# Old output form for the first eight groups, earlier scores for the next batch, and filler matmuls in the head of an inducing-point attention + PReLU expert kernel

## The chip, the cores and the metric

The kernel runs on one core of one Trainium2 chip. The metric is the device time of one execution in microseconds (us). The engines are named as in the profile: PE (TensorE matmuls), PEld (TensorE weight loads), DVE (VectorE), ACT (ScalarE), POOL (GpSimd), SP (SyncE, which here only issues DMAs). A name such as `ring<-rep,hW` means that an instruction writes tile `ring` and reads `rep` and `hW`.

## The reference, cut to what matters

```python
B, N, m, C = (4, 12480, 32, 128)          # x is (B, N, C), inducing is (m, C)
def mab(q, kv):
    s = scale * (q @ kv.transpose(0, 2, 1))
    a = exp(s - s.max(-1)); a /= a.sum(-1)
    return a @ kv
h = mab(I, x)                             # 32 inducing points look at 12480 tokens
x = mab(x, h).reshape(B * N, C)           # every token looks at the 32 points
hid = x @ w_in                            # 128 -> 2048
g = max(hid, 0) + alpha * min(hid, 0)     # PReLU, one alpha for each of the 2048
out = g @ w_out                           # 2048 -> 128, float32
```

## The kernel before, in words

**Tiling.** A batch of 12480 tokens is six supergroups of 2048 tokens and a remainder of 192. A supergroup is four groups of 512, so a batch has 25 groups, and each group passes through four slots `j` (the remainder through two). I write (b, g) for group g of batch b and (b, g, j) for a slot. There are 392 slots in all, and the main loop at the end of the kernel takes them in order. `base = 25 * b` is the number of a batch's first group.

**One slot.** `fill` issues four matmuls that use 32 rows of the array each (`ring<-rep,hW`: the unnormalised attention weights of 512 tokens, kept in `rep`, times the product of the points and `w_in`, kept in `hW`) into four of six PSUM banks called `ring`. ACT (line 470) and DVE (line 472) evict these four banks with a ReLU into `gt`; which engine takes which bank is decided ahead by `make_plan`, a beam search with a cost for every instruction. After that the second matmuls of the slot before are issued by `mm2` into one of two accumulators `acc`. The linear part of the PReLU comes from two small matmuls for a pair of groups (`linear`).

**Two output forms.** `turned(b, g)` chooses between them. In the turned form `mm2` issues four matmuls that stream 512 tokens through weights `W1`, and the result has channels on the partitions. `turn` then transposes blocks on DVE into `yT` (line 563), sixteen DMAs for a supergroup that POOL issues (line 572) shuffle `yT` to `yq`, POOL multiplies by the reciprocal row sums `rd` (line 579) and issues the DMA to `out` (line 589). POOL's sixteen shuffles and four such closings wait in a list `moves`, from which the main loop takes two in a slot. In the old form `mm2` issues sixteen matmuls that load 128 tokens of `gt` as weights and stream 128 columns of `W1`; the tokens are on the partitions at once, and `finish` needs one DVE multiplication (line 548, tile `obe`) and one DMA to `out`. Before the change the old form is used for the last supergroup of the last batch and for the four remainders.

**The next batch's first attention** is interleaved as tasks placed with `at(slot, fn, j)`. For each supergroup u of batch n: `a_load` (POOL issues a casting DMA to `xn`, line 133), `a_xpose` (SP issues a DMA transpose `xT<-xn`, line 158), `a_scores` (PE: `ring<-xT,IT`; ACT: exponential to `e1`; SP: DMA transpose `e1T<-e`, line 281) and `a_accum`, the pooling (PE: sixteen matmuls `ring<-xn,e1T`; DVE adds them to `hacc`). The group in which scores are issued is `t`, the pooling comes at `t + d`, and the load and the transpose at `k` and `k + 1`:

```python
if b == 0:
    k, t, d = (1, 3, 4, 5, 7, 9, 11)[i], (8, 9, 11, 13, 15, 16, 17)[i], 2
else:
    k, t, d = base + (-8, -5, -3, -2, 1, 4, 7)[i], base + (0, 2, 4, 7, 10, 13, 16)[i], 3
```

The index i runs over the supergroups in the order 0, 1, remainder, 2, 3, 4, 5. `e1` and `e1T` come from a pool of two buffers.

**Order.** `pin` chains every instruction to the one before it on its engine, so each engine works in the order in which the code is written, and so does each engine's DMA queue. SP's queue holds, in one order, the transposes of `xn`, those of `e1`, and the copies `e2d<-e` and `rep<-e2d` that spread a supergroup's attention weights.

**The head.** Batch 0's first attention runs ahead of the main loop in halves of a supergroup: PE transposes (`p_xpose`), scores (`p_scores`) and pooling (`p_pool`) into columns 0 to 31 of `acc` 0. Then follow `p_sums`, `p_h`, `p_scale` (row sums and `hT`), `b_scores_pe`, `h_weights` and `b_scores`, which make the first group's `rep` and `hW`.

Of the kernel before, what the change touches and what calls it, by code (L numbers as in the profile page):

```python
# [15 lines left out]
P = 128  # L16
NB = 4
GRP = P * NB
NQ = 4
# [5 lines left out]
def kernel(  # L25
# [11 lines left out]
    bf16 = mybir.dt.bfloat16  # L37
# [5 lines left out]
    NS = N // SUP  # L43
# [31 lines left out]
    gt_pool = ctx.enter_context(tc.tile_pool(name="gtp", bufs=4))  # L75
    head_pool = ctx.enter_context(tc.tile_pool(name="headp", bufs=3))
    rep_pool = ctx.enter_context(tc.tile_pool(name="repp", bufs=3))
    rd_pool = ctx.enter_context(tc.tile_pool(name="rdp", bufs=4))
    dram = ctx.enter_context(
        tc.tile_pool(name="e2d", bufs=3, space=bass.MemoryType.DRAM)  # L80
# [124 lines left out]
    def p_scores(st, u, i):  # L205
        blocks = p_blocks(st, u, i)
        pp, nb = (PR, JR) if u == NS else (P, 2 * NB)
        ps = bank()
        for k, (xt, _) in enumerate(blocks):
            mm(ps[:pp, k * M : (k + 1) * M], xt, IT[:])  # L210
        e1t = head_pool.tile([P, 2 * NB, M], bf16, name="e1t", tag="e1t")
        pin(nc.scalar.activation(  # L212
            out=e1t[:pp, :nb, :].rearrange("p k m -> p (k m)"), in_=ps[:pp, : nb * M],
            func=EXP, scale=scale,
        ))
        st.e1T[u, i] = e1t

    def p_pool(st, u, i, first=False, last=False):
        blocks = p_blocks(st, u, i)
        pp, nb = (PR, JR) if u == NS else (P, 2 * NB)  # L220
        e1t = st.e1T.pop((u, i))
        step = min(4, nb)
        for k in range(0, nb, step):
            mm(
                den[: step * M, :], e1t[:pp, k : k + step, :].rearrange("p k m -> p (k m)"),
                ones[:pp, :], start=(first and k == 0), stop=(last and k + step == nb),
                skip_group_check=True,
            )
        for k, (_, xk) in enumerate(blocks):
            mm(  # L230
                pool, xk, e1t[:pp, k, :], start=(first and k == 0),
                stop=(last and k == nb - 1), skip_group_check=True,
            )
        if u == NS or i == 1:
            st.xn.pop(u)

    def p_sums(st):
        et = work.tile([P, 1], f32, name="et", tag="et")
        pin(nc.vector.tensor_scalar_mul(out=et[:], in0=den, scalar1=1.0 / scale))
        return et  # L240

    def p_scale(st, et):
        ps = bank()
        mm(ps[:, 0:1], fold[:], et[:])
        st.rs = const.tile([P, 1], f32, name="rs")
        st.sc = st.rs
        pin(nc.vector.reciprocal(out=st.rs[:], in_=ps[:, 0:1]))
# [23 lines left out]
    def a_scores(st, u):  # L271
        ps = bank()
        if u < NS:
            for q in range(NQ):
                mm(ps[32 * q : 32 * q + 32, :], IT[:], st.xT[:, u, q, :])
            e1 = work.tile([P, GRP], bf16, name="e1", tag="e1")
            pin(nc.scalar.activation(  # L277
                out=e1[:], in_=ps[:], func=EXP, scale=scale, accum_out=st.es[:, u : u + 1]
            ))
            e1T = work.tile([P, NB, P], bf16, name="e1T", tag="e1T")  # L280
            pin(nc.sync.dma_start_transpose(out=e1T[:], in_=e1[:]))
        else:
            mm(ps[0:M, :REM], IT[:], st.xTr[:].rearrange("c j p -> c (j p)"))
            pin(nc.scalar.activation(
                out=e1r[:, :, :PR],
                in_=ps[0:M, :REM].rearrange("m (j p) -> m j p", j=JR),
                func=EXP, scale=scale, accum_out=st.es[0:M, u : u + 1],
            ))
            e1T = work.tile([P, JR, M], bf16, name="e1Tr", tag="e1Tr")
            pin(nc.sync.dma_start_transpose(  # L290
                out=e1T[:], in_=e1r[:].rearrange("m j p -> m (j p)")
            ))
        st.e1T[u] = e1T
# [88 lines left out]
    def b_rep(st, s, q0=0):  # L382
        nq, w = (NQ, GRP) if s < NS else (1, REM)
        rep = rep_pool.tile([P, nq, w], bf16, name="rep", tag="rep" if s < NS else "repr")
        dv = st.d.pop(s)[:].rearrange("(q i) t -> i q t", q=nq)
        for r in range(4):
            pin(nc.sync.dma_start(out=rep[32 * r : 32 * r + 32, q0:], in_=dv[:, q0:]))
        for q in range(q0, nq):
            st.rep[s * NQ + q] = rep[:, q, :]


    def b_scores_pe(st, q):
        if q == 0:
            st.rep0 = rep_pool.tile([P, NQ, GRP], bf16, name="rep", tag="rep")
        ps = bank()
        mm(ps[:], st.hT4[:], st.xT[:, 0, q, :])
        pin(nc.scalar.activation(
            out=st.rep0[:, q, :], in_=ps[:], func=EXP, scale=scale_of(st)
        ))
        st.rep[q] = st.rep0[:, q, :]  # L400
# [23 lines left out]
        return (P, NB, 1) if g < NS * NQ else (PR, JR, 2)  # L424

    def turned(b, g):
        return g < NS * NQ and (b, g // NQ) != (B - 1, NS - 1)

    def acc_of(b, g):
        return accs[(b * NG + g) % 2]  # L430
# [238 lines left out]
    def w_scale(dst, fac):  # L669
        for j in range(NJ):  # L670
            f = fac[:, j::NJ]
            fb = bass.AP(tensor=f.tensor, offset=f.offset, ap=[f.ap[0], f.ap[1], [0, C]])
            pin(nc.gpsimd.tensor_tensor(
                out=dst[:, j::NJ, :], in0=w_out_f[:, j::NJ, :], in1=fb, op=MULT
            ))
# [28 lines left out]
    for i in range(n):  # L704
        if i + 1 < n:
            p_xpose(st, *halves[i + 1], last=i + 2 == n)
        p_scores(st, *halves[i])
        if i > 0:
            p_pool(st, *halves[i - 1], first=i == 1)
        if i == 3:  # L710
            alphas()
            w_scale(W1, om_al)
            w_scale(AW, alT)
    p_pool(st, *halves[n - 1], last=True)
    et = p_sums(st)
    p_h(st)
    p_scale(st, et)
    b_scores_pe(st, 0)
    h_weights(st, first=True)
    b_scores(st, 0)  # L720
    b_rep(st, 0, 2)
    w_inT()

# [8 lines left out]
    def at(slot, fn, j=1, cost=None, narrow=False):  # L732
        tasks.setdefault((slot, j), []).append((fn, cost))
        if narrow:
            narrows.add((slot, j))

    def late_finish():
        linear(st, [0])
        finish(st, 0)

    at(0, lambda: b_scores_pe(st, 1), 1, (240, "A", 480))
    at(0, lambda: b_den(st, 0), 2, (130, "D", 250))
    at(1, w_amat, 2, (950, "D", 250))
# [4 lines left out]
    for b in range(B):  # L748
        base = b * NG
        for s in range(1, NS + 1):  # L750
            g = base + (s * NQ - 6 if s > 1 else -2 if b else 0)
            at(g, lambda b=b, s=s: b_scores(states[b], s), 3, (215, "A", 490), narrow=True)
            at(g + 1, lambda b=b, s=s: b_rep(states[b], s), 1 if g + 1 == base - 1 else 3)
            g = base + s * NQ - 4
            at(g + 2, lambda b=b, s=s: b_den(states[b], s), 2, (130, "D", 250))
        if b + 1 < B:
            n = b + 1

            def begin(n=n):
                states[n] = new_batch(n)  # L760

            for i, u in enumerate(order):
                if b == 0:
                    k, t, d = (1, 3, 4, 5, 7, 9, 11)[i], (8, 9, 11, 13, 15, 16, 17)[i], 2
                    turn_at = k + 1, 1
                else:
                    k, t, d = base + (-8, -5, -3, -2, 1, 4, 7)[i], base + (0, 2, 4, 7, 10, 13, 16)[i], 3
                    turn_at = k + 1, 1 if k + 1 == base - 1 else 3
                if i == 0:
                    at(k, begin)  # L770
                at(k, lambda n=n, u=u: a_load(states[n], u), 3 if i == b == 0 else 1)
                at(turn_at[0], lambda n=n, u=u: a_xpose(states[n], u), turn_at[1])
                at(t, lambda n=n, u=u: a_scores(states[n], u), 0, (215, "A", 680), narrow=True)
                at(t + d, lambda n=n, u=u: a_accum(states[n], u), 3, (200, "D", 220), narrow=True)
            k = base + NG - 6
            at(k, lambda n=n: h_sum(states[n]))
            at(k, lambda n=n: h_den(states[n]), 2, (250, "D", 500))
            at(k + 1, lambda n=n: h_transpose(states[n]), 1, (300, "D", 250))
            at(k + 1, lambda n=n: h_weights(states[n]), 3, (215, "D", 600), narrow=True)
            at(k + 2, lambda n=n: b_scores(states[n], 0), 1, (215, "A", 490), narrow=True)  # L780
            at(k + 2, lambda n=n: h_linear(states[n]), 3, (80, "D", 250))
            at(k + 3, lambda n=n: b_rep(states[n], 0), 0)
            at(k + 3, lambda n=n: b_den(states[n], 0), 1, (130, "D", 250))
# [120 lines left out]
```

## Time and profile before

| | us |
|---|---|
| median of 11 runs | 603.37 |
| lowest and highest run | 601.56 and 607.9 |
| the profiled execution, its own time | 605.04 |
| span of the profile (first to last instruction) | 603.3 |

The profiled execution lies 1.7 us above the median, and 1.7 us of its time lie outside the span. The profile's page gives the busy share of each engine over the span:

| engine | busy us | share |
|---|---|---|
| PE | 564.0 | 93% |
| ACT | 512.9 | 85% |
| DVE | 501.7 | 83% |
| POOL | 365.9 | 61% |
| PEld | 218.0 | 36% |

The mean granted clock of PE is 0.982. The DMA queue of POOL (software_dynamic) has 62.39 MB and takes 44.1% of the sixteen DMA engines' span, the queue of SP (hardware_dynamic) 29.94 MB and 23.9%. A share is a mean over stages: the slices of the page show PE at 90% or more in most of them and lower in a few, and it is these few that a reader should look up in the windows, the list of waits and the chain of the work that ended last.

### The profile page before, as it was taken

Reading aid. Unit: us, or ns where it says so; the run is one execution under the profiler, and the core shown is the slowest. Engines: PE = TensorE matmul, PEld = TensorE weight load, DVE = VectorE, ACT = ScalarE, POOL = GpSimd, SP = SyncE. Lnnn points to the kernel's source line nnn. Section 1 sums busy time; section 2 is a strip of 40 time slices with the busy share of each in tenths; the row PEclk is TensorE's granted clock in tenths of the full one; section 3 lists DMA queues with packets and bytes.
Section 4 is the critical chain, followed back from the end, with each engine's and each line's share of the span. In section 5 each row is a group of like instructions: output and inputs, shape, how many; then the busy total and the mean of one; then the engine's idle time right before and its main releaser. Section 6 shows DMA issues by size and latency. Waiting matters only on the chain.

```text
span 603.3 us, 14402 instructions
## 1 busy us (share of the span) xinstructions
PE 564.0 (93%) x5233; PEld 218.0 (36%) x5310; DVE 501.7 (83%) x841; ACT 512.9 (85%) x1015; POOL 365.9 (61%) x629
## 2 busy tenths in 40 slices
PE   4999995999999799999999899999999999999997
PEld 4533331333343233333334233333334333333366
DVE  3579984888879689989888788998988899899996
ACT  2579994988998699899899689999888998999886
POOL 6713573665757466488646365667865764865854
PEclk9899997999999899999999999999999999999999
DMA  9759989878789895856697978865444443453443
GB/s 199 179 120 171 192 166 165 151 190 149 158 168 191 179 184 136 175 166 162 154 180 185 144 191 179 154 175 154 127 118 131 128 136 128 114 140 123 117 104 134
DMA packets 93638, 93.76 MB, mean 155 GB/s; under 512 B 61328, under 2 KB 76960, under 8 KB 93568
## 3 DMA queue, kind: packets, MB, share of 16 engines
q0 software_dynamic: 24224, 62.39, 44.1%
q1 hardware_dynamic: 69200, 29.94, 23.9%
q8 instruction: 41, 0.67, 0.5%
q10 hardware_dynamic: 144, 0.52, 0.3%
q14 instruction: 29, 0.24, 0.2%
HBM read 40.20 MB, written 28.75 MB: 114 GB/s over the span
## 4 chain that ended last, share of the span: by engine, by line
PE 85%; DMA 7%; issue 3%; ACT 2%; DVE 2%; SPq 0%; DVEq 0%; ACTq 0%
PE acc L99 58%; PE ring L99 26%; DMA e1T<-e 6%; ACT gt L470 2%; PE ring L187 1%; DVE gt L472 1%; DMA ind_f<-in_inducing_dram 1%; DVE fr L332 0%; DVE xT L193 0%; DVE hW L263 0%; DVE yT L563 0%; DVE xn L695 0%; ACT xT L195 0%; DVE obe L548 0%; SPq L609 0%
## 5 line engine op out<-in xcount | busy, mean ns | idle before, releaser
L470 ACT ACTIVATE gt<-ring 128x512 bf16<-128x512 f32 (+1 forms) x927 | 481.9, 600 | 69.9 <-ACT gt L470 27.2
L472 DVE TENSOR_SCALAR gt<-ring 128x512 bf16<-128x512 f32 x641 | 415.3, 683 | 66.4 <-PE ring L99 56.5
L99 PE MATMUL acc<-gt,W 128*128 128x512 bf16 (+1 forms) x2188 | 370.8, 387 | 10.8 <-issue 9.8
L572 POOL DMA_DIRECT2D yq<-yT x368 | 180.6, 499 | 91.4 <-DMA xn<-in_x_dram 39.5
L99 PEld LDWEIGHTS <-W 128*128 128x128 bf16 (+1 forms) x2264 | 124.6, 98 | 155.0 <-issue 67.4
L99 PE MATMUL ring<-rep,hW 32*128 32x512 bf16 (+1 forms) x1600 | 167.4, 382 | 0.5 <-DVE hW L263 0.2
L579 POOL TENSOR_TENSOR ob<-yq,rd 128x512 f32<-128x512 f32 x92 | 97.0, 1055 | 77.7 <-DMA yq<-yT 76.2
L99 PEld LDWEIGHTS <-hW 32*128 32x128 bf16 x1600 | 44.4, 91 | 164.9 <-issue 160.0
L563 DVE STREAM_TRANSPOSE yT<-acc 128x512 f32<-128x512 f32 x92 | 65.2, 709 | 6.2 <-PE acc L99 5.8
L589 POOL DMA_DIRECT2D out_dram<-ob x92 | 53.7, 584 | 27.4 <-POOL ob L579 27.1
L133 POOL DMA_DIRECT2D xn<-in_x_dram x28 | 15.6, 561 | 21.4 <-ACT gt L470 18.6
L99 PE MATMUL acc<-W,gt 128*128 128x128 bf16 (+1 forms) x384 | 25.6, 220 | 0.0
L99 PEld LDWEIGHTS <-gt 128*128 128x128 bf16 (+1 forms) x384 | 21.9, 106 | 4.1 <-issue 3.6
L99 PE MATMUL ring<-xn,e1T 128*32 128x128 bf16 x288 | 7.5, 226 | 13.4 <-DMA e1T<-e 13.1
L99 PE MATMUL acc<-rep,hA 32*128 32x512 bf16 x92 | 17.6, 375 | 0.0
L308 DVE TENSOR_TENSOR hacc<-ring,hacc 128x128 f32<-128x128 f32 x18 | 5.1, 282 | 10.6 <-PE ring L99 10.6
L212 ACT ACTIVATE e1t<-ring 128x256 bf16<-128x256 f32 (+1 forms) x13 | 4.8, 372 | 10.2 <-PE ring L99 10.1
L193 DVE COPY xT<-ring 128x1024 bf16<-128x1024 bf16 (+1 forms) x12 | 8.0, 670 | 4.7 <-PE ring L187 4.3
L99 PEld LDWEIGHTS <-e1T 128*32 128x32 bf16 x288 | 5.2, 97 | 17.2 <-DMA e1T<-e 14.3
L369 ACT ACTIVATE e<-ring 128x512 bf16<-128x512 f32 x18 | 11.2, 620 | 0.0
L99 PE MATMUL ring<-xT,hT 128*32 128x512 bf16 (+1 forms) x97 | 10.3, 393 | 0.7
L277 ACT ACTIVATE e<-ring 128x512 bf16<-128x512 f32 x18 | 10.9, 603 | 0.0
(92 smaller groups left out, 140.8 us busy)
## 6 DMA issues: line engine op xcount, KB each, us to landing
yq<-yT POOLq DMA_DIRECT2D x368, 64.0 KB, 4.0
out_dram<-ob POOLq DMA_DIRECT2D x92, 256.0 KB, 2.8
rep<-e2d SPq DMA_DIRECT2D x92, 128.0 KB, 3.1
xn<-in_x_dram POOLq DMA_DIRECT2D x18, 512.0 KB, 6.8
e2d<-e SPq DMA_DIRECT2D x24, 128.0 KB, 2.7
xn<-in_x_dram POOLq DMA_DIRECT2D x10, 256.0 KB, 8.7
w_out_f<-in_moe_w_out_dram POOLq DMA_DIRECT2D x4, 256.0 KB, 10.8
out_dram<-obe SPq DMA_DIRECT2D x4, 256.0 KB, 2.7
```

What stands on the lines that cost most here:

```text
L99: return pin(nc.tensor.matmul(o, lhsT, rhs, start=start, stop=stop, **kw))
L133: bi = pin(nc.gpsimd.dma_start(out=xn[:, i * w : (i + 1) * w, :], in_=src[:, i * w : (i + 1) * w, :]))
L187: pin(nc.tensor.transpose(tp[:, k * P : (k + 1) * P], xn[:, q, j * C : (j + 1) * C], ident[:]))
L193: pin(nc.vector.tensor_copy(out=dst, in_=tp[:, :w]))
L277: pin(nc.scalar.activation(out=e1[:], in_=ps[:], func=EXP, scale=scale, accum_out=st.es[:, u : u + 1]))
L369: pin(nc.scalar.activation(out=e2[:], in_=ps[:], func=EXP, scale=scale_of(st)))
L470: pin(nc.scalar.activation(out=gt[:, r, :w], in_=ps[:, :w], func=RELU))
L472: pin(nc.vector.tensor_relu(gt[:, r, :w], ps[:, :w]))
L563: pin(nc.vector.transpose(out=yT[:, :, q, :, :].rearrange("p a j c -> p j a c"), in_=acc[:].rearrange("p j (a c) -> p j a c", a=4),))
L572: pin(nc.gpsimd.dma_start(out=yq[32 * a : 32 * a + 32, k], in_=yT[32 * k : 32 * k + 32, a]))
L579: pin(nc.gpsimd.tensor_tensor(out=ob[:].rearrange("p j (k c) -> p j k c", k=4), in0=yq[:, :, q].rearrange("p k j c -> p j k c"), in1=bass. ...
L589: pin(nc.gpsimd.dma_start(out=out[t0 : t0 + SUP, :].rearrange("(p q j) c -> q p j c", q=NQ, j=NB)[q], in_=ob[:],))
```

## The change

Four things change. First, `turned` is false for the first eight groups of batch 0 (two supergroups), so they take the old output form. Second, `t` moves two to three groups forward and `d` grows by two, so that pooling stays where it was, up to a group; `k` is as before. Third, `e1` and `e1T` come from a pool of their own with four buffers. Fourth, `warm` issues filler matmuls of 384 columns (identity times part of `xT`) into the columns of `acc` 0 that the head does not use; nothing reads them. Nine are issued: one ahead of the last two halves' pooling each, one after the pooling, two after `p_scale`, two after the first `b_scores`, and two in slot (0, 0, 0).

```diff
+    e1_pool = ctx.enter_context(tc.tile_pool(name="e1p", bufs=4))
...
+    def warm(st, n=1):
+        for _ in range(n):
+            mm(
+                accs[0][:, 1:, :].rearrange("p k c -> p (k c)"), ident[:],
+                st.xT[:, 0, 0, : 3 * P], start=False, stop=False, skip_group_check=True,
+            )
...
-            e1 = work.tile([P, GRP], bf16, name="e1", tag="e1")
+            e1 = e1_pool.tile([P, GRP], bf16, name="e1", tag="e1")
...
-            e1T = work.tile([P, NB, P], bf16, name="e1T", tag="e1T")
+            e1T = e1_pool.tile([P, NB, P], bf16, name="e1T", tag="e1T")
...
     def turned(b, g):
-        return g < NS * NQ and (b, g // NQ) != (B - 1, NS - 1)
+        if g == NS * NQ or (b, g // NQ) == (B - 1, NS - 1):
+            return False
+        return b > 0 or g >= 2 * NQ
...
         p_scores(st, *halves[i])
+        if i == n - 1:
+            warm(st)
...
+    warm(st)
     p_pool(st, *halves[n - 1], last=True)
+    warm(st)
     et = p_sums(st)
     p_h(st)
     p_scale(st, et)
+    warm(st, 2)
     b_scores_pe(st, 0)
     h_weights(st, first=True)
     b_scores(st, 0)
+    warm(st, 2)
...
+    at(0, lambda: warm(st, 2), 0)
...
-                    k, t, d = (1, 3, 4, 5, 7, 9, 11)[i], (8, 9, 11, 13, 15, 16, 17)[i], 2
+                    k, t, d = (1, 3, 4, 5, 7, 9, 11)[i], (6, 7, 9, 10, 12, 14, 15)[i], 4
...
-                    k, t, d = base + (-8, -5, -3, -2, 1, 4, 7)[i], base + (0, 2, 4, 7, 10, 13, 16)[i], 3
+                    k, t, d = base + (-8, -5, -3, -2, 1, 4, 7)[i], base + (-3, 0, 2, 4, 7, 10, 13)[i], 5
```

## The prediction

> **What bounds the kernel now.** I read the page's chain first. PE holds 85% of it, so away from a few places PE's own work sets the time; DMA has 7%, which is about 42 us of a 603.3 us span and too much for a load at the start alone. Next I read PE's list of waits (in total, times, longest):
>
> ```profile
> PE 85%; DMA 7%; issue 3%; ACT 2%; DVE 2%; SPq 0%; DVEq 0%; ACTq 0%
> ...
> PE ring L99 <- DMA e1T<-e: 13.1, 4, 6.1
> PE acc L99 <- issue: 9.8, 61, 0.3
> PE ring L648 <- DVE ind_b L645: 6.3, 1, 6.3
> ```
>
> The 6.3 us are the start and stay. The 13.1 us in four waits are for `e1T`: the pooling of the next batch stands in PE's order and its transposed weights have not landed. The windows show what one such wait does (PE, PEld, DVE, ACT and POOL busy, PE clock, DMA share, GB/s), and the last two lines show the head's end:
>
> ```profile
> 92.00:96.00 4.00, 2.29 (x15) 0.61 (x13) 2.88 (x5) 3.75 (x8) 0.13 (x1) 1.00 1.12 166
> 96.00:100.00 4.00, 0.00 (x0) 0.00 (x0) 0.00 (x0) 0.00 (x0) 0.37 (x1) 0.59 1.14 92
> 100.00:104.00 4.00, 3.27 (x38) 1.33 (x40) 0.92 (x3) 0.61 (x2) 2.69 (x3) 0.56 0.79 195
> ...
> 28.00:32.00 4.00, 4.00 (x26) 0.95 (x28) 1.67 (x4) 1.37 (x3) 3.71 (x4) 0.52 0.48 111
> 32.00:36.00 4.00, 3.82 (x41) 1.28 (x35) 3.66 (x7) 3.57 (x8) 0.00 (x0) 1.00 0.51 111
> ```
>
> All engines stop for 6.1 us, the clock falls to half, and PE then works at half speed until 103.5. At 28 to 32 PE is full and yet DVE and ACT are under half busy: that is half clock, not useful work. Why is `e1T` late? SP's queue, in order of time:
>
> ```profile
> 85.47 2.31 SPq L158 DMA_TRANSPOSE xT<-xn  x1
> 87.87 1.81 SPq L281 DMA_TRANSPOSE e1T<-e  x1
> 95.61 3.87 SPq L158 DMA_TRANSPOSE xT<-xn  x1
> ```
>
> Its scores ran at 78.5, but SP stood at line 158 for a load of `xn` that landed at 85.5; then `e1T` took 12.5 us to land, at 100.4. The waits at 201.5 (scores at 176.9: 24.6 us) and 345.2 (321.0: 24.1 us) are the same case. The loads are late because POOL issues them behind its shuffles: that of batch 1's i = 4, due in group 7 (67.3), went out at 78.1.
>
> **What the Trainium skill says.** "TensorE: Matmul & The Clock Gate", Part 1 (The HAM clock gate): one idle window of about 3.4 us halves PE's clock and a busy one restores it. The trace agrees: half clock at 25.0 to 31.8, 96.7 to 103.5, 202.5 to 205.9 and 345.9 to 349.3, the last three right at the `e1T` waits; sixteen matmuls that take 0.86 us take 1.71 there. "DMA: Bandwidth & Descriptors", Queues, rings and completion order: an engine consumes a ring's descriptors in order and takes turns between rings. The trace fits it: 12.5 us directly behind a transpose of `xn`, with POOL's loads and shuffles beside it, against a median of 5.2. "TensorE", Part 2 (step 1): weight loads are pulled ahead of running matmuls, which matters for the old form. Priced below from the last supergroup.
>
> **The change part by part.** Group lengths are the times from one group's first `ring<-rep,hW` to the next one's.
>
> *Scores earlier.* Loads, transposes and pooling keep their groups up to one, so only the distance grows. In the old clock the new distance from scores to pooling is 26 to 38 us for all 21 tasks, and the longest time from scores to landing was 24.6 us, itself long because SP waited for a load; in the new order that `e1T` (batch 2, i = 0, now in group (0, 22), 162) stands on SP ahead of the transposes at 175.7 and 188.9. So all four waits should go. Worth, with like groups as measure: group 11 took 12.95 against 5.7 (-7.2), group 15 6.5 against 5.7 (-0.8), groups (1, 3) and (1, 4) 9.06 + 6.85 against 5.58 + 5.78 (-4.55), (2, 3) and (2, 4) 8.61 + 6.62 against the same (-3.9). Sum **-16.4 us**. As a check: 13.1 of waits and half of the clock's 3.1 + 3.4 + 3.4 us at work are 18.0; a little is caught up by DVE and ACT meanwhile. The same matmuls and exponentials are issued, so PE, ACT and DVE have no more work. SP's eighteen transposes of 1.25 us move past copies of `rep`, which are issued five groups ahead of use: hidden.
>
> *What is late next.* Scores need `xT`. With old landings and new places the margin is 4.0 us at least (batch 2, i = 1 and 6: 4.0 and 4.1; batch 3, i = 6: 4.7), but for one: batch 1, i = 6 is 4.3 us short, because its load left at 108.7 behind the second supergroup's shuffles and closings, which this change removes; due at 91, it lands in time. POOL's turnaround of a supergroup is 23.4 to 26 us where PE needs 22 to 24, so without PE's stalls POOL falls some 3 us further behind in batches 1 and 2, less what it gains at the start. I take **+0.4 us** (0 to +8 as bounds).
>
> *Old form, eight groups.* The last supergroup shows its price: groups 21 and 23 of batch 3 took 5.31 us against 5.19 for groups 17 and 19, and
>
> ```profile
> 552.60:574.20 21.60, 21.21 (x151) 7.06 (x153) 20.15 (x33) 19.24 (x38) 14.38 (x24) 1.00 0.39 114
> 574.20:596.00 21.80, 21.80 (x327) 16.03 (x326) 19.94 (x33) 19.34 (x38) 12.64 (x22) 1.00 0.40 114
> ```
>
> PE is full in the second line; the first holds more scores and sums. Eight groups by 0.12 are 1.0; with the linear part in small pieces I take **+1.2** (0.5 to 3). DVE changes 8 x 709 ns (line 563) for 8 x 686 ns (line 548): nothing. POOL loses 32 shuffles of 0.5 us, 8 multiplications of 1.06 us and their waits, and the DMA engines 32 x 64 KB; none of this is on PE's path, its use is that batch 1's loads go out on time. `narrow` does nothing in the old form; at the four or five slots concerned PE's work is equal.
>
> *Fillers.* Nine by 384 columns. A 512-column matmul takes 0.216 us in a row of them (0.86 for four), so one is 0.16, 1.4 in all, twice that at half clock. In the program's waits the pair after `p_scale` takes over the wait for DVE's read of `acc` 0 that `b_scores_pe` had, so these two only delay it (0.3); the others fill waits for the exponential, for `et` and for `hW`. Cost **+0.4**. Gain: group 0 took 8.34 us with the clock at half until 31.8. At full clock its PE work is 4 x 0.41 + 3 x 0.86 + about 0.6 = 4.8, its start has to wait one round of evictions (1.3), so 6.5 to 7: **-1.6**. The window that failed (21.6 to 25.0) holds some 1.5 us of real array time by my count of columns, seven to nine fillers make it 2.6 to 2.9: likely enough, not certain, since the window's phase is free. Bounds -2.5 to +1.4.
>
> Sum: -16.4 + 0.4 + 1.2 + 0.4 - 1.6 = **-16.0**. From the profiled 605.0 (span 603.3 and 1.7 around it) that is 589.0; the median stands 1.7 below the profiled run, so I predict **587.4**.
>
> **The rivals.**
> *The clock stays cold in the head* (the fillers cost and bring nothing): 587.4 + 1.6 to 2.6 = 589 to 590. For it: the free phase; against: nearly doubled array time.
> *The wait moves from `e1T` to `xT`*: scores three groups earlier meet a transpose whose load POOL issued late. For it: margins of 4 us and POOL at its limit; against: POOL starts two supergroups lighter. A 4 us deficit in one or two batches with half clock after it gives +3 to +8: 590 to 596.
> *Slower*: the same queue, further. A stall shifts everything behind it, so the deficits of a batch don't add; they are its largest. To outweigh 16 us, batches 2 and 3 must each have scores 8 us ahead of `xT`, that is loads 12 us later against PE than before. That would be POOL's lateness (at most 8.4 us now) more than doubled, and would decide only if shuffles, not PE, set the pace from batch 1 on: 606 to 610. Against it: POOL is 61% busy, and from 440 us on it starts within 1 us of its data.
> *It does not do what it says*: one early `e1T` (batch 1, i = 1, behind the transpose of 65.7) still lands after its pooling, though with 26 us it shouldn't: +2, inside the range.
>
> **How the numbers follow.** Forecast 0.62, cold head 0.15, `xT` waits 0.16, slower 0.04, something small against the gain 0.03. The forecast's own range is 584.5 to 590; the two middle rivals reach 596, and a full recovery of the 18.0 with a cheaper old form gives 583.5. Range 583.5 to 595.5. A difference under 0.3% (1.8 us) is about what a measurement can't tell from none; within it only partial mishaps end: 0.03. Faster 0.93, slower 0.04.
>
> **What would show it.** No line `e1T<-e` in PE's waits; no clock under 1.00 after 32 us but at the very end; group 11 at about 5.7; PEclk 1.00 at 25 to 32 and group 0 under 7; groups 0 to 7 0.12 to 0.2 longer than turned ones; loads of batch 1 within a slot or two of their groups. Wrong would be: a PE wait on `xT<-xn`, a clock drop beside it, or the main loop's groups all longer.

## The result, and the profile after

| | before | after |
|---|---|---|
| median of the runs, us | 603.78 (47 runs) | 596.85 (12 runs) |
| lowest and highest run, us | 599.22, 611.61 | 588.31, 604.12 |
| ratio, after to before | | 0.983 (95%: 0.9798 to 0.9863) |
| profiled execution, us; its span | 605.04; 603.3 | 598.35; 596.6 |

The ratio of 0.983 stands for 10.3 us (8.3 to 12.2) of 603.8. The changed kernel's executions scatter over 16 us, and for both kernels the ratio, here and below, uses only executions within 1.5% of the fastest one (seven of these twelve), so that it shows a larger gain than the medians of all runs do, which lie 6.9 us apart. The forecast was 16.0 us.

PE's list of waits in the profile after (in total, times, longest) has no line for `e1T` any more. Two others stand in its place:

```profile
PE ring L100 <- DMA xT<-xn: 4.4, 2, 3.4
PE ring L100 <- DMA rep<-e2d: 3.2, 3, 1.8
```

The windows (PE, PEld, DVE, ACT and POOL busy, PE clock, DMA share, GB/s) show the head first and then the two places of these waits:

```profile
24.00:28.00 4.00, 3.85 (x42) 1.66 (x41) 3.16 (x6) 3.66 (x7) 4.00 (x5) 1.00 0.28 82
28.00:32.00 4.00, 4.00 (x62) 2.85 (x62) 3.30 (x7) 3.33 (x7) 3.91 (x4) 1.00 0.58 130
308.00:312.00 4.00, 0.85 (x4) 0.18 (x2) 0.00 (x0) 1.48 (x3) 0.65 (x2) 1.00 1.17 212
312.00:316.00 4.00, 3.62 (x27) 2.40 (x29) 1.82 (x3) 1.21 (x4) 3.36 (x5) 0.61 0.51 146
386.00:390.00 4.00, 1.67 (x38) 0.66 (x36) 2.80 (x6) 2.17 (x4) 1.83 (x4) 1.00 1.38 200
390.00:394.00 4.00, 2.62 (x25) 0.85 (x27) 0.31 (x1) 1.03 (x3) 0.76 (x1) 0.67 0.38 69
```

In the head the clock stays at 1.00, and DVE and ACT are busy for 3.3 of the 4 us at 28 to 32, where they were under half busy before. At 308 and at 388 PE starves and then works at half clock for a while, as it did at the old `e1T` waits.

The chain that ended last tells where these waits come from. Before, PE held 85% of it. Now:

```profile
PE 51%; DMA 25%; POOL 16%; issue 5%; ACT 1%; DVE 1%; POOLq 0%; SPq 0%
PE acc L100 35%; PE ring L100 15%; DMA yq<-yT 12%; DMA xn<-in_x_dram 11%; POOL ob L589 7%; POOL yq L582 5%; POOL out_dram L599 4%; DMA xT<-xn 1%; PE ring L188 1%; ACT gt L480 1%; DMA ind_f<-in_inducing_dram 1%; DVE xT L194 0%; DVE gt L482 0%; POOLq L589 0%; DVE xn L705 0%
```

From about 127 us up to the wait at 388 the chain runs along POOL's queue. POOL in order of time, with the idle time ahead of an instruction and what ended it in brackets, and below it the transpose on SP that needs the last load:

```profile
342.63 1.04 POOL L589 TENSOR_TENSOR ob<-yq,rd 128x512 f32<-128x512 f32 x1 [9.97 <-DMA yq<-yT]
...
350.44 0.56 POOL L134 DMA_DIRECT2D xn<-in_x_dram  x1
...
366.81 1.04 POOL L589 TENSOR_TENSOR ob<-yq,rd 128x512 f32<-128x512 f32 x1 [4.72 <-DMA yq<-yT]
...
374.62 0.56 POOL L134 DMA_DIRECT2D xn<-in_x_dram  x1
```

```profile
383.18 2.24 SPq L159 DMA_TRANSPOSE xT<-xn  x1
```

POOL stands for ten microseconds at the first multiplication of a supergroup, because that supergroup's sixteen shuffles have not landed. Behind it in the same queue stand the next shuffles and the load of `xn`. The load of 374.62 (batch 3, i = 6) is due in group (2, 7), which began at 353.5; its transpose landed at 391.0, and the scores that wanted it stood ready from 387.7. The second line of shares shows that the shuffles are only half of what the chain waits for: at a shuffle behind a load POOL often stands until that load has landed (`yq L582 <- DMA xn<-in_x_dram` in POOL's list of waits, 29.0 us in nine waits, against 76.5 in 21 for the closings). No shuffle reads `xn`; why it waits for the load was not looked into.

The sum closes. Against the like groups of a kernel without waits (`e8_pad` below), the remainder ahead of group (2, 0) takes 4.51 us instead of 2.66 and group (2, 0) 9.68 instead of 5.78, group (1, 13) 6.49 instead of 5.49, and (2, 13) 10.45 instead of 5.49: 1.8 + 3.9 + 1.0 + 5.0 = 11.7 us. The span of that kernel is 585.1, 11.5 us shorter.

### The profile page after: what moved, and what is told of

It reads as the page before. It is cut to its first block, busy times and chain, and to the rows that moved or that the text cites. A ratio compares the mean times of both kernels' runs of the same rounds, so it can differ in the third digit from the quotient of the medians.

```text
span 596.6 us, 15012 instructions
## 1 busy us (share of the span) xinstructions
PE 562.7 (94%) x5565; PEld 237.5 (40%) x5631; DVE 506.6 (85%) x852; ACT 509.7 (85%) x1004; POOL 341.4 (57%) x589
## 4 chain that ended last, share of the span: by engine, by line
PE 51%; DMA 25%; POOL 16%; issue 5%; ACT 1%; DVE 1%; POOLq 0%; SPq 0%
PE acc L100 35%; PE ring L100 15%; DMA yq<-yT 12%; DMA xn<-in_x_dram 11%; POOL ob L589 7%; POOL yq L582 5%; POOL out_dram L599 4%; DMA xT<-xn 1%; PE ring L188 1%; ACT gt L480 1%; DMA ind_f<-in_inducing_dram 1%; DVE xT L194 0%; DVE gt L482 0%; POOLq L589 0%; DVE xn L705 0%
## 5 line engine op out<-in xcount | busy, mean ns | idle before, releaser
L482 DVE TENSOR_SCALAR gt<-ring 128x512 bf16<-128x512 f32 (+1 forms) x652 | 422.1, 683 | 64.4 <-PE ring L100 54.8
L100 PE MATMUL acc<-gt,W 128*32 128x512 bf16 (+1 forms) x1975 | 335.9, 382 | 9.8 <-issue 9.2
L582 POOL DMA_DIRECT2D yq<-yT x336 | 164.8, 500 | 73.8 <-DVE yT L573 29.2
L100 PEld LDWEIGHTS <-W 128*32 128x32 bf16 (+1 forms) x2040 | 112.7, 97 | 140.4 <-issue 60.8
L589 POOL TENSOR_TENSOR ob<-yq,rd 128x512 f32<-128x512 f32 x84 | 88.6, 1055 | 77.9 <-DMA yq<-yT 76.5
L100 PE MATMUL acc<-W,gt 128*128 128x128 bf16 (+1 forms) x896 | 60.6, 221 | 0.0
L100 PEld LDWEIGHTS <-gt 128*128 128x128 bf16 (+1 forms) x896 | 51.5, 103 | 9.9 <-issue 9.0
L134 POOL DMA_DIRECT2D xn<-in_x_dram x28 | 15.6, 563 | 27.8 <-ACT gt L480 24.6
L567 POOL DMA_DIRECT2D out_dram<-obe x11 | 6.0, 541 | 32.0 <-DVE obe L558 32.0
L213 ACT ACTIVATE e1t<-ring 128x256 bf16<-128x256 f32 (+1 forms) x13 | 4.8, 372 | 10.2 <-PE ring L100 10.0
L100 PE MATMUL ring<-xT,IT 128*32 128x512 bf16 x72 | 7.2, 390 | 4.4 <-DMA xT<-xn 4.4
L188 PE MATMUL ring<-ident,xn 128*128 128x128 bf16 x96 | 8.8, 249 | 0.9 <-DVE xn L705 0.9
```

What stands on the lines that cost most here:

```text
L100: return pin(nc.tensor.matmul(o, lhsT, rhs, start=start, stop=stop, **kw))
L134: bi = pin(nc.gpsimd.dma_start(out=xn[:, i * w : (i + 1) * w, :], in_=src[:, i * w : (i + 1) * w, :]))
L188: pin(nc.tensor.transpose(tp[:, k * P : (k + 1) * P], xn[:, q, j * C : (j + 1) * C], ident[:]))
L482: pin(nc.vector.tensor_relu(gt[:, r, :w], ps[:, :w]))
L582: pin(nc.gpsimd.dma_start(out=yq[32 * a : 32 * a + 32, k], in_=yT[32 * k : 32 * k + 32, a]))
L589: pin(nc.gpsimd.tensor_tensor(out=ob[:].rearrange("p j (k c) -> p j k c", k=4), in0=yq[:, :, q].rearrange("p k j c -> p j k c"), in1=bass. ...
```

## The experiments

Every kernel was timed beside the kernel before, in five rounds. I first took the change apart.

**Scores alone.** The diff is the two lines with `t` and `d` and the pool `e1_pool`, on the kernel before.

> The kernel before with the earlier scores and the pool of four e1/e1T buffers alone; turned output everywhere as before, no fillers. Theory A (the earlier scores free PE of the e1T waits, 16.4 us, but POOL's queue of shuffles and loads then falls behind and gives part of it back as waits on xT and rep; the old form in batch 0 only delays that): no wait on e1T, waits on xT already in batch 1 because POOL starts with two supergroups more, 594 to 600 us, slower than the whole change by 1 to 5 us. Theory B (the old form is what costs the missing 6 us, POOL has no part): 586 to 590 us and no wait on xT. Head: clock at half for 3.4 to 6.8 us after 25 us in both.

Measured: median 604.06, ratio 0.9985 (0.9954 to 1.0016), no difference. In its profile no `e1T` wait is left, and this stands instead:

```profile
PE ring L100 <- DMA xT<-xn: 10.8, 2, 9.2
PE ring L100 <- DMA rep<-e2d: 1.6, 3, 1.1
```

```profile
116.00:120.00 4.00, 0.00 (x0) 0.00 (x0) 0.71 (x2) 0.44 (x1) 2.44 (x5) 1.00 0.92 91
120.00:124.00 4.00, 0.00 (x0) 0.00 (x0) 0.00 (x0) 0.00 (x0) 1.97 (x4) 0.52 1.23 199
124.00:128.00 4.00, 3.14 (x25) 1.01 (x27) 0.54 (x1) 1.21 (x4) 1.42 (x2) 0.50 0.50 119
```

That is the one case in which the prediction found `xT` 4.3 us short, the last load of batch 1. Theory A is right in kind, but the median lies above its 594 to 600 us: the loss is larger than it said, since the half clock after the wait lasted 10.2 us, until 130.4, and group 15 took 17.36 us.

**Old form alone.** The diff is `turned` alone.

> The kernel before with the old output form for the first two supergroups alone. My price says +1.2 us on PE (0.12 to 0.15 us for each of eight groups) and that POOL issues batch 1's loads on time, so the e1T waits of batch 0 (6.9 us, and 1 us of half clock) go, while those of batches 1 and 2 (3.5 and 2.7 us) stay: 596 to 600 us. If the old form is only a cost on PE, 604.5 to 605.5 us with the waits of batch 0 still there.

Measured: median 597.85, ratio 0.9894 (0.9869 to 0.9919), 6.4 us faster. The profile has one `e1T` wait left, in batch 1:

```profile
PE ring L99 <- DMA e1T<-e: 6.3, 1, 6.3
```

The waits of batch 0 are gone though no scores were moved, and batch 1's loads go out within 2.6 us of their slots (before, up to 17.6 us late). So taking work off POOL repairs `e1T` as well; the old form also takes 32 transfers of 64 KB off the DMA engines, and this run doesn't separate the two. That batch 2's wait is missing too says little: the next profile shows two waits instead of four as well, in a kernel that changes nothing after the head.

**Fillers alone.** The diff is `warm` and its calls.

> The kernel before with the nine filler matmuls alone. My sum says -1.2 us: head longer by 0.4, group 0 of batch 0 6.0 to 7 us against 8.34, clock at 1.00 from 25 to 32 us. Rival (the clock drops in the head all the same, or group 0 is bound by its evictions): 604 us, no difference, or +0.4. Later waits on e1T stay as before in both.

Measured: median 602.8, ratio 0.9994 (0.9963 to 1.0024): no gain that this run can tell. In the profile group 0 took 5.84 us instead of 8.34 and the clock stayed up, as expected; but 9.0 us of `e1T` waits follow, in which 1 us can vanish. The forecast of 1.2 us lies inside the interval, so this run doesn't decide.

**The change without the old form.** The diff puts `turned` back.

> The whole change but for the old output form: earlier scores, four buffers and fillers. Theory A: as e1_scores with the head's gain of 1 us, 593 to 599 us; waits on xT and rep in all three batches, more in sum than the 7.6 us of the changed kernel's profile. Theory B: 585 to 588 us, faster than the whole change.

Measured: median 602.4, ratio 0.9955 (0.9921 to 0.9989), slower than theory A's 593 to 599 us. Theory B, which blamed the old form's cost on PE, is out. The wait is again the last load of batch 1, 10.3 us long:

```profile
PE ring L100 <- DMA xT<-xn: 10.8, 2, 10.3
PE ring L100 <- DMA rep<-e2d: 2.2, 4, 0.8
```

So early scores bring nothing by themselves, the old form 6.4 us, and both together with the fillers 10.3. By the medians of all runs these are 1.3, 7.5 and 6.9 us, so what early scores add to the old form is small and hangs on which executions are counted. The profiles show in what way they depend on it: without the old form batch 1's last load goes out 17.7 us late, with it 2.3. The next four kernels ask what exactly is late on POOL in the changed kernel.

**Loads earlier.**

```diff
-  k, t, d = base + (-8, -5, -3, -2, 1, 4, 7)[i], ...
+  k, t, d = base + (-8, -6, -5, -4, -1, 2, 5)[i], ...
```

> The changed kernel with the loads of batches 2 and 3 (and with them their transposes) one to two groups earlier: k = base + (-8, -6, -5, -4, -1, 2, 5) instead of (-8, -5, -3, -2, 1, 4, 7); scores and pooling as they are. Theory P (POOL issues in order, so loads stand behind shuffles and closings that are 10 to 16 us late; the lost time is the load's place in that queue): the waits on xT at i = 6 and the wait on rep ahead of batch 2's first group go, 587 to 590 us, a ratio to the kernel before of 0.970 to 0.976. Theory D (the sixteen DMA engines are full around the start of a batch, whatever the order): crowding the loads moves the wait elsewhere, 594 to 600 us, ratio 0.98 to 0.99.

Measured: median 593.01 (589.53 to 599.41), ratio 0.9795 (0.9732 to 0.9859). In the profile (587.8 us span) no `xT` wait is left, and 0.5 us for `rep`. The execution with the profile agrees with theory P; the others scatter up to 599, and the interval reaches into both theories' numbers. POOL's lateness (from the last `yT` of a supergroup to its first shuffle) still reached 15.0 us. Not decisive.

**Scores of i = 3 to 6 one group later.**

```diff
-  base + (-3, 0, 2, 4, 7, 10, 13)[i], 5
+  base + (-3, 0, 2, 5, 8, 11, 14)[i], (5, 5, 5, 4, 4, 4, 4)[i]
```

> The changed kernel with the scores of i = 3 to 6 in batches 2 and 3 one group later, so only two groups earlier than before (t = base + (-3, 0, 2, 5, 8, 11, 14), pooling unchanged). Both theories give i = 6 one more group (5.6 us) of margin over the 1.3 and 3.7 us by which it was short: no wait on xT, -4.5 to -6 us against the changed kernel in its slower executions. The rep wait at the start of batch 2 (some 4 us of group (2, 0)) stays, because nothing in that place changes: 590 to 594 us, ratio 0.976 to 0.983. If waits on xT come back at other places or on e1T, the margin was not the cause.

Measured: median 592.13 (590.7 to 595.23), ratio 0.9811 (0.976 to 0.9862). As expected, no wait on `xT`, and group (2, 0) still takes 9.79 us with 2.6 us of waits on `rep`. The margin was the cause of the `xT` waits; the `rep` wait is another one.

**Old form in two more supergroups.**

```diff
+        if g // NQ == NS - 1 and b < 2:
+            return False
         return b > 0 or g >= 2 * NQ
```

> The changed kernel with the old output form for the last supergroup of batches 0 and 1 too, whose shuffles fall together with the loads at the start of the next batch. Price on PE: 2 x 0.5 to 0.6 us. Theories P and D both say that POOL then starts batches 1 and 2 without lateness (under 5 us at their first supergroups instead of 10 to 13): no waits on xT and rep, 589 to 592 us, ratio 0.974 to 0.979. If POOL's lateness has no part in the loss, 598 us.

Measured: median 587.57 (586.97 to 588.13), ratio 0.9727 (0.9678 to 0.9777), faster than expected. No waits on `xT` or `rep`, POOL's lateness 6.0 us at most, and the scatter of the runs is gone.

**Closings four slots later.** This one takes no work away. It only changes the order in POOL's list:

```diff
+        for _ in range(8):
+            moves.append(lambda: None)
         for k in range(NQ):
             moves.append(lambda k=k: leave(k))
```

> The changed kernel with eight empty entries in POOL's list between a supergroup's sixteen shuffles and its four closings, so that the closings come four slots (5.2 us) later and loads and other issues pass ahead of them. No work is taken away. Theory P: POOL no longer stands still for its own shuffles to land (25.1 us in five waits between 168 and 310 us), its lateness falls under 5 us, 587 to 591 us, ratio 0.970 to 0.978. Theory D: the shuffles themselves land late because the DMA engines are full, the same waits on xT stay, 594 to 600 us.

Measured: median 587.0 (586.65 to 587.54), ratio 0.972 (0.9676 to 0.9764). This is theory P. Theory D as it was stated, the same waits whatever the order because the DMA engines are full, is out: the same bytes move. How much of the gain is POOL's order and how much is transfers that collide less isn't separated, since the entries also move the closings' transfers to `out`, and the median time from issue to landing of a shuffle falls from 3.2 to 2.6 us. POOL's wait for its own shuffles, over the whole span, in the changed kernel and in this one:

```profile
POOL ob L589 <- DMA yq<-yT: 76.5, 21, 10.0
```

```profile
POOL ob L589 <- DMA yq<-yT: 45.5, 19, 6.3
```

The waits of shuffles for a load fall from 29.0 to 10.2 us. The greatest lateness falls from 16.2 to 8.1 us, not under the 5 that theory P gave. What matters to PE falls further: the loads for i = 6 in batches 2 and 3 went out 20.0 and 19.6 us after their slots in the changed kernel, and 3.1 and 4.2 here. PE's list has nothing but the start and small things left:

```profile
PE acc L100 <- issue: 8.9, 56, 0.2
PE ring L660 <- DVE ind_b L657: 6.2, 1, 6.2
PE ring L188 <- DVE xn L707: 0.9, 1, 0.9
PE ring L100 <- DVE et L332: 0.8, 2, 0.4
```

**The same entries on the kernel before.** If POOL's order is the root, the change's other parts may not be needed.

> The kernel before with the eight empty entries ahead of the closings alone; scores, pooling and output forms as before, no fillers. Theory P1 (the old e1T waits had the same root: loads late on POOL, so SP stands at a transpose of xn and e1T behind it is late): most of the 13.1 us of e1T waits go without moving any scores, 588 to 595 us. Theory P2 (two or three groups between scores and pooling are too few whatever POOL does): e1T waits stay, 599 to 604 us.

Measured: median 589.01 (587.34 to 591.52), ratio 0.9772 (0.9715 to 0.9828). All four `e1T` waits are gone with scores and pooling where they were:

```profile
PE ring L650 <- DVE ind_b L647: 6.1, 1, 6.1
PE ring L187 <- DVE xn L697: 0.9, 1, 0.9
PE ring L99 <- DVE et L324: 0.8, 2, 0.4
PE ring L99 <- DVE es L122: 0.4, 1, 0.4
```

Here POOL's greatest lateness hardly moved (8.0 us against 8.4): it is the loads that come earlier, that of batch 1, i = 4, 2.3 us after its slot instead of 9.5, and i = 6 3.0 instead of 17.6. The distance of two to three groups was enough, though with little to spare: in two poolings of batch 1 `e1T` landed 1.2 and 2.2 us ahead of its use.

**The entries without the old form.**

> The changed kernel with the empty entries and without the old output form (turned form in the first two supergroups). If the old form's gain was only that it made POOL lighter, the entries stand in for it, no wait on xT is left and PE saves the price of eight groups in the old form: 585.5 to 586.5 us, 0.5 to 1.5 under the 587.0 of e8_pad. If batch 1's last load still stands behind the second supergroup's shuffles: a wait on xT at i = 6 of batch 1, 588 to 597 us.

Measured: median 589.62 (586.59 to 593.46), ratio 0.9786 (0.9719 to 0.9853). The time is that of the second case, with a wait at i = 6 of batch 1:

```profile
PE ring L100 <- DMA xT<-xn: 6.7, 1, 6.7
```

The cause is not the one that was expected. POOL issued this load 3.0 us after its slot, and SP its transpose behind it:

```profile
92.52 0.57 POOL L134 DMA_DIRECT2D xn<-in_x_dram  x1
105.28 5.57 SPq L159 DMA_TRANSPOSE xT<-xn  x1
```

The load took 9.2 us to land, the transpose 13.1, and the one between them in SP's queue, `e2d`, 7.3 us; in `e8_pad` the load took 6.0 and the transpose 7.5. So here the transfers themselves are slow, in a kernel with two supergroups' shuffles more to move, and a part of theory D is right for this place; which transfers slow the others isn't shown. The six runs scatter from 586.6 to 593.5 us, and the fastest was granted the full clock throughout, so the wait doesn't come in each.

Groups 0 to 7 of batch 0 take 46.04 us in this profile and 47.17 in `e8_pad`: the old form costs PE 1.1 us.

**The entries without fillers, and without two of them.**

> The changed kernel with the empty entries and without the nine fillers. Without waits later in the kernel nothing can swallow what the head gains: if the head's 2 us (group 0 8.3 us without, 6.0 with fillers, less 0.4 to 0.6 for a later start) reach the end, 588.5 to 589.5 us. If the gain is swallowed, 587.0.

> The changed kernel with the empty entries and without the two fillers after p_scale, which only delay b_scores_pe by my reading of the waits. If that reading is right and seven fillers keep the clock up: 586.6 to 586.8 us, group (0, 0) starts 0.2 to 0.3 us earlier. If the pair is needed for the clock: half clock at 25 us and 588 to 589 us.

Measured: without fillers median 588.02 (586.67 to 588.91), ratio 0.975 (0.9693 to 0.9806); without the pair after `p_scale` 586.89 (586.32 to 587.03), ratio 0.9731 (0.9684 to 0.9779). Against 587.0 with all nine, and 586.89 with seven in the same rounds as these, the fillers bring about 1.0 us, in medians of six runs whose ranges overlap a little. It is a mixture: three of the six runs without fillers lie at 586.7 to 587.7 with a granted clock of 0.997 to 0.999, three at 588.4 to 588.9 with 0.992. The profile, of one of the first three, shows what is gained there: group 0 takes 7.34 us without and 6.0 with them, and starts at 24.6 without and 25.2 with. Without the pair the clock stays up too, and the head starts at 25.2 as with it, so the pair neither helped nor cost anything that shows.

## Why the prediction was right or wrong

**Right.** The four `e1T` waits went, the group lengths that the prediction took as measure came out (group 11 at 5.53, (1, 3) at 5.19, (2, 3) at 5.19), no clock drop is left at the old places, and batch 1's loads went out two slots behind their place, 2.3 to 2.6 us. The old form was put at +1.2 and costs 1.1. The fillers were put at -1.2 net and bring about -1.0. (Their gain was put at group 0 in 6.5 to 7 us; the prediction's own terms, 4.8 and 1.3, make 6.1, and it measured 6.0.) Taken without new waits the sum came out: `e8_pad`, which has none, stands at 587.0 and the forecast was 587.4. But the earlier scores, to which the sum gave 16.4, were not needed for that: `e9_pad_before` loses the same four waits without them.

**Wrong: "What is late next", +0.4 us.** It measured 11.5 us in the profiled execution, and the ratio leaves about 6 us of the forecast 16 unfound. Three things in that step failed.

First, its mechanism was right (POOL falls behind once PE no longer stalls) but its size, "some 3 us", was not. POOL's lateness at a supergroup was 8.4 us at most before and 16.2 after. The step comes at one place:

```profile
179.16 2.94 POOL L582 DMA_DIRECT2D yq<-yT  x6 [4.36 <-DMA xn<-in_x_dram]
...
195.45 1.04 POOL L589 TENSOR_TENSOR ob<-yq,rd 128x512 f32<-128x512 f32 x1 [9.62 <-DMA yq<-yT]
```

Over these two waits the lateness grows from 2.8 to 10.2 us, and it stays at 9 or more until 421. A stall of PE lets POOL catch up: in `e1_scores` the lateness was 9.1 us ahead of PE's wait of 9.2 us and 0.3 after it. The margins of 4.0 to 4.7 us that the prediction listed were computed in the old clock, with such stalls in it. Batch 3, i = 6, listed at 4.7, came out 3.4 short.

Second, "copies of `rep`, which are issued five groups ahead of use: hidden" does not hold for the first supergroup of a batch. Its `rep` is issued three groups ahead, and in SP's order it stands behind the transpose of i = 1, which waits for a load:

```profile
302.49 2.15 SPq L159 DMA_TRANSPOSE xT<-xn  x1
304.74 2.76 SPq L395 DMA_DIRECT2D rep<-e2d  x4
```

SP waited 10.9 us for that load, and PE wanted the last pieces of `rep` from 308 on. This is a place of the slower rival's mechanism that the rival did not name; its price there, 1.8 + 3.9 us, is half of what was lost.

Third, the prediction treated POOL's relief as a side effect ("its use is that batch 1's loads go out on time"). The experiments turn this round: the old form alone, with its relief of POOL, brings 6.4 us, early scores alone nothing, and a mere change in POOL's order 2.3% to the kernel before. In the kernel before and in the changed one, the waits on `e1T`, `xT` and `rep` are one wait, that of a load behind POOL's closings, seen at three places of SP's queue: the same eight entries take all of them away. `e10_pad_no_old` shows that a load which leaves on time can still come late.

**The rivals.** The cold head did not come. The move of the wait from `e1T` to `xT` did, as far as 3.4 and 1.0 us, with half clock after the longer one; a wait on `xT<-xn` with a clock drop beside it was the prediction's own sign of being wrong. Its 590 to 596 us hold what the ratio gives, 593.5, which the forecast's own 584.5 to 590 does not; the median of all runs, 596.85, lies above both and above the whole range. The slower rival's condition, POOL's lateness more than doubled, was nearly met (16.2 against 8.4); it wasn't slower, which fits what was argued there, that the deficits of a batch don't add, but no run tests this. With the old form left out the wait on `xT` took almost all of the gain of the earlier scores. The early `e1T` of batch 1 that might still have been late was not.

What stays open is why the shuffles of one supergroup land 10 us after issue at some places and 3 to 4 at others. No run isolates which of the transfers beside them does it.

## What to carry to other kernels

When waits for different transfers appear at different places, follow each back through the queues to the first instruction that was late on its own engine; a gap that was closed here by moving the consumer showed up at the next consumer. A queue that issues loads should not hold an instruction that waits for its own transfers right ahead of them: moving the four closings of a supergroup by four slots, alone, gave a ratio of 0.977 (0.9715 to 0.9828), the whole change 0.983 (0.9798 to 0.9863); these intervals overlap, so nothing shows the large change to be better than the small one. Margins read from a trace with stalls in it can be too large, because the stalled engine's partners catch up during the stall, as POOL did here.

## What the hardware showed that I had not expected

The scatter of the runs is a sign of such waits. The changed kernel's twelve runs span 15.8 us: the two at 588.3 and 591.3 us were granted a mean clock of 0.999, those from 595.8 us up 0.990 to 0.994, so these two can hardly have had the waits that are followed by half clock. `e5_loads` spans 9.9 us, while `e8_pad` and `e7_more_old`, with no wait on a transfer of more than 0.6 us after the head, span 0.9 and 1.2 us in six runs each. `e9_pad_before` has none in its profile either and spans 4.2 us; margins of 1.2 and 2.2 us leave room for one in other executions.

A wait of PE costs more than its length. After 9.2 us of waiting in `e1_scores` the clock was at half from 120.2 to 130.4, some six of these microseconds with PE already at work, and in `e4_no_old` from 115.5 to 129.2. In the head without fillers the half clock lasted 6.8 us in the profile before and 3.4 us in that of `e11_pad_no_fill`, so what fillers can bring differs from execution to execution.
